# A normalised linear-attention layer and a token/channel mixer on one core: first loads in whole tiles, beta2's column beside the first channel product, q's split in two pieces, the last chunk in two halves

## The chip, the core and the metric

The kernel runs on one core of one Trainium2 chip. A core has a tensor engine (PE, with its weight loads listed apart as PEld), a vector engine (DVE), a scalar engine (ACT), GpSimd (POOL), and SyncE (SP), which here only issues DMAs; 16 DMA engines move the data. The metric is the device time of one execution in microseconds (us); the median of several executions counts.

## The reference, cut to what matters

Eight batches (`b`), 8 heads of 64 columns, 576 tokens. First an attention without softmax, with a normalised output, then a residual mixer over tokens and over channels:

```
kv  = einsum('bhsd,bhse->bhde', k, v)             # 64 x 64 per batch and head
o   = einsum('bhsd,bhde->bhse', q, kv)
x   = o / sqrt(mean(o*o, -1) + 1e-6) * g_norm     # heads side by side: 576 x 512 per batch
u   = x + lam * einsum('ts,bsd->btd', w_tok, alpha1 * x + beta1)
a2  = alpha2 * u + beta2
out = u + lam * (relu(a2 @ w_ch1) @ w_ch2)        # w_ch1: 512 x 2048, w_ch2: 2048 x 512
```

All inputs and the output are float32. The big products run in bf16.

## The kernel before

**One program, ordered by a planner.** The kernel is a list of operations, each with an engine (or two to choose from), a cost that the author wrote beside it, and the keys that it reads and writes. `plan` (L122) schedules the list eight times with due times for the first products of batch 0 and 1 (`mark`, L1277), keeps the best, and `emit` (L351) writes every engine's instructions in that order with the waits that the keys call for. Each engine runs its own list strictly in that order, so an instruction that waits holds all behind it. The author's costs decide the order alone; they have no part in the running time. Where the schedule sees PE idle before the first channel product, it puts in a **filler** (`warm`, L1341): a 128x512 matmul on zeros, whose result nobody reads. A filler is an ordinary instruction and is run whether or not PE would in fact have waited there.

**PSUM** has eight banks of 512 float32 columns; a tile takes one or two of them, and an operation that opens a tile waits for the readers of the tile before it in that bank.

**Batch 0, the start.** `load_first` (L508) loads k and v of four heads at a time: for k and for v two DMAs, each into 64 partitions (two heads, nine token rows of 64 floats to a partition, 2304 bytes in a run). `load_q` brings q's 512 first tokens of four heads, `load_tail` (L500) the last 64 tokens of all eight heads. All go through SP's queue, in the order of L1115 to L1124, with `w_tok` behind them. `kv_first` (L601) multiplies k by v in float32 on 64x64 tiles of PE, `qt_first` (L623) turns q by a product with the identity, and `qkv_groups(0)` (L745, its float32 form `f32`, L767) multiplies q by kv two heads at a time. Then come the normalisation (ACT: square L799, root L804; DVE: sum L801, reciprocal L807, scaling L820, and L824 for the token product's operand; POOL: the factor g_norm, L828), the turned `w_tok` (L1151), the token product (`tok_first`, L894), and `ut_pe` (L927), which turns u and scales it by alpha2 (L949, L950).

**The channel products.** `ch1_groups` (L976) does for each of 16 column blocks `fj` four 128x512 matmuls (even batches, L988) or eight 128x320 ones (odd batches with the tails of two batches, L1002), and ACT takes the result out of PSUM with relu (L978) and the bias `hb`, one column per `fj`. `hb` is beta2 times w_ch1: `load_w` (L1233) makes it as soon as a quarter of w_ch1 is there, with 16 matmuls of one moving column (L1256), each with its own weight load, and one copy by ACT (L1260). `ch2_groups` (L1015) multiplies by w_ch2 in parts of four matmuls (L1025); after a chunk's fourth part DVE adds u (L1035) and SP stores the chunk (L1038; the tail chunk of two batches in two DMAs, L1042). The last batch does its chunks in the order 0, 1, 2, 3, tail.

**q of the later batches.** `split_q` (L540) splits q into two bf16 parts: ACT copies it (L562, listed under L490, the line of `copy`), DVE subtracts (L564). For batches 2 to 7 that is one instruction of 128x2048 on each engine and one for the tail. `qt_dma` (L567) then turns the five token chunks by DMA transposes in SP's queue (L573), and `kv_groups` (L659) makes kv from float32 products (L673, L683), which ACT and DVE take out of PSUM (L700, L705, L708). `matmul_held` (L387) is a matmul that keeps the weights of the matmul before it: `qkv_groups` uses the pair L764 and L390 on 64 columns each.

Of the kernel before, what the change touches and what calls it, by code (L numbers as in the profile page):

```python
# [13 lines left out]
NB = 8  # L14
# [381 lines left out]
def bass_transnormer_attn__then__resmlp_affine_kernel(  # L396
# [15 lines left out]
    with ExitStack() as stack:  # L412
# [47 lines left out]
        wst = hst[:, 0:2304].rearrange("p (c s) -> p c s", c=4)  # L460
        wst2 = hst[0:64, 2304:2880]

        def nine(tile, a, g):
            return tile[64 * g:64 * g + 64, a].rearrange("p h c d -> p (h c d)")[
                :, 0:1152].rearrange("p (h c d) -> p h c d", h=2, c=9)

        def flat(ap):
            return ap.rearrange("p h d -> p (h d)")
# [31 lines left out]
        def load_tail(tile, key, src, b, lo, eng="SP"):  # L500
            P.op(eng, 0.6, lambda e: e.dma_start(
                tile[lo:lo + 64, :, :], src[b, :, 512:576, :].rearrange("h s d -> s h d")),
                w=[key], dma_us=0.75)

        HALVES = (slice(0, 4), slice(4, 8))
        ALL = (slice(0, 8),)

        def load_first(a):  # L508
            for key, src, tile in (("kf", k, kf), ("vf", v, vf)):
                for g in range(2):  # L510
                    P.op("SP", 0.45, lambda e, src=src, tile=tile, g=g: e.dma_start(
                        nine(tile, a, g).rearrange("p h c d -> p h (c d)"),
                        src[0, 4 * a + 2 * g:4 * a + 2 * g + 2].rearrange(
                            "h (p c) d -> p h (c d)", c=9)),
                        w=[(key, a)] if g == 0 else [(key + "g", a)], dma_us=1.05)

        def load_kv(b, go=()):
            j = (b + 1) % 2
            for tile, tl, src, n in ((kf, kft, k, "kf"), (vf, vft, v, "vf")):
                P.op("SP", 0.6, lambda e, tile=tile, src=src: e.dma_start(  # L520
                    tile[:, j].rearrange("p h c d -> p h (c d)"),
                    src[b, :, 0:512, :].rearrange("h (p c) d -> p h (c d)", c=4)),
                    r=go, w=[(n, j), (n + "g", j)], dma_us=3.8)
# [77 lines left out]
        def kv_first():  # L601

            def group(a):
                t = P.ptile(2)

                def f(e):
                    for c in range(9):
                        for h in (0, 2, 1, 3):
                            g, r = h // 2, slice(64 * (h % 2), 64 * (h % 2) + 64)
                            m = e.matmul(t.ap(r)[:, g, 0:64], nine(kf, a, g)[:, h % 2, c, :],  # L610
                                         nine(vf, a, g)[:, h % 2, c, :],
                                         start=(c == 0), stop=(c == 8), skip_group_check=True)
                    return m
                P.op("PE", 1.8, f, r=[(n, a) for n in ("kf", "kfg", "vf", "vfg")], w=[t])
# [8 lines left out]
        def qt_first():  # L623

            def pair(pr):
                t = P.ptile(1)

                def f(e):
                    for c in range(4):
                        for h in range(2):  # L630
                            m = e.matmul(t.flat(slice(64 * h, 64 * h + 64))[  # L631
                                :, 128 * c:128 * c + 128], qf[:, 2 * pr + h, c, :], ident[:],
                                start=True, stop=True)
                    return m
                P.op("PE", 0.95, f, r=["ident", ("qf", pr // 2)], w=[t])
# [3 lines left out]
            def tail(a):  # L639
                t = P.ptile(1)  # L640

                def f(e):
# [6 lines left out]
                P.op("PE", 0.28, f, r=["ident", "qft0"], w=[t])  # L649
# [95 lines left out]
        def qkv_groups(b):  # L745

            def group(cs, hs):
# [19 lines left out]
                def f32(e):  # L767
                    a = h0 // 4
                    for i, c in enumerate(cs):
                        for j in range(2):  # L770
                            mm = e.matmul(  # L771
                                t.flat(rows)[:, 256 * i + 128 * j:256 * i + 128 * j + 128],
                                qt32[:, 2 * a + j, 128 * c:min(128 * c + 128, 576)],
                                kv32[:, 2 * a + j, :], start=True, stop=True)
# [152 lines left out]
        def ut_pe(b):  # L927


            def group(cs, dj):  # L930
# [14 lines left out]
                al = ab2[:, 0, dj:dj + 1]  # L945

                def g(e):
                    if e is nc.scalar:
                        return e.activation(o, t.flat()[:, 0:n], ACT.Identity, scale=al)  # L949
                    return e.tensor_scalar(out=o, in0=t.flat()[:, 0:n], scalar1=al,  # L950
                                           scalar2=None, op0=ALU.mult)
# [24 lines left out]
        def ch1_groups(b):  # L976
            def relu(t, src, dst, fj, n):
                o = P.op("ACT", act_us(n) + 0.09, lambda e: e.activation(  # L978
                    dst, src(), ACT.Relu, bias=hb[:, fj:fj + 1]),
                    r=[t, ("hb", fj // 4)], w=[("ht", fj)])  # L980
                mark(b, 0, fj + 1.5, o)

            def even(fj):
                t = P.ptile(1)

                def f(e):
                    for dj in range(4):
                        m = e.matmul(t.flat(), w1[:, dj, 128 * fj:128 * fj + 128],  # L988
                                     a2t[:, dj, 0:512], start=(dj == 0), stop=(dj == 3))
                    return m  # L990
                o = P.op("PE", 0.87, f, r=[("w1", fj // 4)] + [("a2t", i) for i in range(4)],
                         w=[t])
                mark(b, 0, fj, o)
                relu(t, lambda: t.flat(), ht[:, fj, 0:512], fj, 512)

            def odd(fj):
                t = P.ptile(2)

                def f(e):
                    for i in range(2):  # L1000
# [8 lines left out]
                mark(b, 0, fj, o)  # L1009
                relu(t, lambda: t.ap()[:, :, 0:320],  # L1010
                     ht[:, fj, :].rearrange("p (a f) -> p a f", a=2), fj, 640)
            for fj in range(16):
                yield lambda fj=fj: (odd if b % 2 else even)(fj)

        def ch2_groups(b):  # L1015
            tiles = {}

            def part(c, n):
                if n == 0:
# [20 lines left out]
                else:  # L1040
                    for i in range(2):
# [3 lines left out]
            nc_ = 5 if b % 2 else 4  # L1045
            order = ([(c, n) for n in range(4) for c in range(nc_)] if b == 0
                     else [(c, n) for c in range(nc_) for n in range(4)])
            for c, n in order:
                yield lambda c=c, n=n: part(c, n)

        prow = xm[0:1, 1, :, :].rearrange("p c d -> p (c d)")
        prow2 = xtl[0:1, 1, :]
# [62 lines left out]
        for i, hs in enumerate(HALVES):  # L1115
            load_first(i)
            load_q(0, hs, False)
            if i == 0:
# [114 lines left out]
        def load_w(i):  # L1233
# [6 lines left out]
            if i < 4:  # L1240
# [9 lines left out]
                t = P.ptile(1)  # L1250

                def f(e):
                    for j in range(4):
                        fj = 4 * i + j
                        for dj in range(4):
                            m = e.matmul(t.flat()[:, j:j + 1], w1[:, dj, 128 * fj:128 * fj + 128],  # L1256
                                         b2c[:, dj:dj + 1], start=(dj == 0), stop=(dj == 3))
                    return m
# [116 lines left out]
```

## Time and profile before

| | us |
|---|---|
| device time, median of 3 (lowest, highest) | 372.38 (371.55, 372.96) |
| device time of the profiled execution | 371.84 |
| its span (first to last instruction) | 370.0 |
| PE busy within the span | 361.4 (98%) |
| DVE / ACT / POOL busy | 200.9 / 161.6 / 82.1 |
| DMA queue of SP | 92,240 packets, 59.41 MB |

The span lies 1.84 us under the device time of the same execution. A matmul's shown length holds its way through the array, so several that follow each other overlap: their pace is read from the starts, or from the chain of waits, which cuts them at the next start. "idle <- X" says how long an engine sat idle and what released it. The stages of a batch follow each other on PE with the next batch's attention laid between the channel products.

### The profile page before, as it was taken

The page shows a single profiled execution, that of the slowest core. Times are in us where ns is not written, and L with a number is a line of the kernel's source. Part 1 is how long each engine was busy: PE and PEld are TensorE (multiplying, and loading weights), DVE is VectorE, ACT ScalarE, POOL GpSimd, SP SyncE. Part 2 cuts the span into 40 slices and gives each one's busy share as a digit, 9 for nine tenths or more (in the row PEclk, how much of TensorE's full clock was granted, in tenths as well). Part 3 has the DMA queues.
Part 4 walks back from the last instruction along what each step waited for, and adds up shares of the span by engine and source line. Part 5 has one row for each costly group of instructions (what it writes and reads, how often), then busy time and mean ns, then how long its engine had stood idle before and what let it go on. Part 6 is the DMA issues. An engine that isn't in the chain of part 4 may idle for free.

```text
span 370.0 us, 7042 instructions
## 1 busy us (share of the span) xinstructions
PE 361.4 (98%) x3153; PEld 207.9 (56%) x2873; DVE 200.9 (54%) x302; ACT 161.6 (44%) x264; POOL 82.1 (22%) x69
## 2 busy tenths in 40 slices
PE   7999999999999999999999999999999999999995
PEld 3787656467754554456654554457654554457642
DVE  2377796982299279715937165925833175720021
ACT  1464886227850187008760188107730186007500
POOL 4043007340064008400341006200620007100000
PEclk9999999999999999999999999999999999999999
DMA  7999999889925893989954399233403110330021
GB/s 183 268 317 310 382 385 308 233 254 181 311 65 128 200 271 100 148 200 300 200 138 113 123 304 186 58 99 85 88 13 101 58 30 1 70 115 3 0 86 58
DMA packets 92295, 59.87 MB, mean 162 GB/s; under 512 B 59549, under 2 KB 82085, under 8 KB 92136
## 3 DMA queue, kind: packets, MB, share of 16 engines
q1 hardware_dynamic: 92240, 59.41, 61.6%
q8 instruction: 24, 0.39, 0.4%
q14 instruction: 7, 0.06, 0.1%
q10 hardware_dynamic: 24, 0.01, 0.0%
HBM read 38.56 MB, written 9.44 MB: 130 GB/s over the span
## 4 chain that ended last, share of the span: by engine, by line
PE 96%; ACT 2%; issue 0%; DVE 0%
PE ps L1025 34%; PE ps L1002 18%; PE ps L988 14%; PE ps L853 8%; PE ps L673 4%; PE ps L1342 3%; PE ps L764 2%; PE ps L390 2%; PE ps L875 1%; PE ps L771 1%; PE ps L905 1%; PE ps L940 1%; PE ps L631 1%; ACT qs L490 1%; ACT ht L978 1%; PE ps L610 1%
## 5 line engine op out<-in xcount | busy, mean ns | idle before, releaser
L1025 PE MATMUL ps<-w,ht 128*128 128x512 bf16 x576 | 129.7, 379 | 0.0
L978 ACT ACTIVATE ht<-ps,hb 128x512 bf16<-128x512 f32 (+1 forms) x128 | 93.4, 740 | 46.2 <-PE ps L1002 38.4
L828 POOL TENSOR_TENSOR xm<-xm,g_bc 128x512 f32<-128x512 f32 (+1 forms) x36 | 49.1, 1364 | 195.7 <-DVE rt L824 193.1
L1025 PEld LDWEIGHTS ps<-w,ht 128*128 128x128 bf16 x576 | 54.6, 98 | 64.3 <-issue 1.2
L1002 PE MATMUL ps<-a2t,w 128*128 128x320 bf16 x512 | 72.0, 299 | 1.4 <-ACT ht L978 1.4
L1002 PEld LDWEIGHTS ps<-a2t,w 128*128 128x128 bf16 x512 | 49.4, 98 | 21.9 <-ACT ht L978 1.9
L988 PE MATMUL ps<-a2t,w 128*128 128x512 bf16 x256 | 58.0, 379 | 0.0
L1035 DVE TENSOR_TENSOR xm<-ps,xm 128x512 f32<-128x512 f32 x32 | 21.7, 687 | 63.1 <-PE ps L1025 63.0
L700 ACT ACTIVATE kvd<-ps 64x128 bf16<-64x128 f32 x28 | 7.6, 271 | 98.0 <-PE ps L683 97.7
L801 DVE TENSOR_REDUCE small<-sq 128x16 f32<-128x1024 f32 (+3 forms) x27 | 25.2, 933 | 32.0 <-ACT sq L799 31.9
L988 PEld LDWEIGHTS ps<-a2t,w 128*128 128x128 bf16 x256 | 24.0, 98 | 26.9
L853 PE MATMUL ps<-rt,wt 128*128 128x512 bf16 x112 | 28.7, 379 | 0.0
L860 DVE TENSOR_TENSOR xm<-ps,xm 128x1024 f32<-128x1024 f32 x14 | 17.0, 1221 | 21.5 <-PE ps L853 21.4
L799 ACT ACTIVATE sq<-ps 128x1024 f32<-128x1024 f32 (+3 forms) x27 | 21.5, 797 | 8.1 <-PE ps L771 4.4
L824 DVE TENSOR_TENSOR rt<-xm,e1g_bc 128x1024 bf16<-128x1024 f32 (+1 forms) x18 | 21.3, 1182 | 0.1
L705 DVE TENSOR_TENSOR kvd<-ps,kvd 64x128 bf16<-64x128 f32 x28 | 8.1, 289 | 24.4 <-ACT kvd L700 23.8
L764 PEld LDWEIGHTS ps<-kvd,qt 128*128 128x128 bf16 x280 | 17.9, 98 | 3.9
L820 DVE TENSOR_TENSOR xm<-ps,small 128x1024 f32<-128x1024 f32 (+1 forms) x18 | 19.8, 1099 | 0.3
L564 DVE TENSOR_TENSOR qs<-qf,qs 128x2048 bf16<-128x2048 f32 (+1 forms) x10 | 17.7, 1787 | 3.1 <-ACT qs L490 3.0
L390 PE MATMUL ps<-kvd,qt 128*128 128x64 bf16 x280 | 19.0, 193 | 0.0
L764 PE MATMUL ps<-kvd,qt 128*128 128x64 bf16 x280 | 19.0, 193 | 0.0
L853 PEld LDWEIGHTS ps<-rt,wt 128*128 128x128 bf16 x112 | 11.0, 98 | 12.9 <-DVE xm L1035 0.2
(103 smaller groups left out, 287.9 us busy)
## 6 DMA issues: line engine op xcount, KB each, us to landing
out_dram<-xm SPq DMA_DIRECT2D x32, 256.0 KB, 2.6
kf<-in_k_dram SPq DMA_DIRECT2D x7, 1024.0 KB, 9.9
vf<-in_v_dram SPq DMA_DIRECT2D x7, 1024.0 KB, 9.7
qf<-in_q_dram SPq DMA_DIRECT2D x7, 1024.0 KB, 7.7
stg<-in_moe_w_ch_dram SPq DMA_DIRECT2D x3, 1024.0 KB, 14.5
kf<-in_moe_w_ch_dram SPq DMA_DIRECT2D x2, 1024.0 KB, 13.8
kf<-in_k_dram SPq DMA_DIRECT2D x4, 288.0 KB, 6.2
vf<-in_v_dram SPq DMA_DIRECT2D x4, 288.0 KB, 7.8
```

The lines of the kernel that those rows point to most:

```text
L390: return pe.add_instruction(mybir.InstMatmult(start_tensor_calc=start, stop_tensor_calc=stop, tile_size=(128, 128), tile_position=(0, 0), ...
L764: e.matmul(o, w, kvd[:, h, 0, :], start=True, stop=False)
L799: P.op("ACT", act_us(64 * m), lambda e: e.activation(sqv, raw(), ACT.Square), r=[t], w=[("sq", sqs)])
L801: P.op("DVE", dve_us(64 * m), lambda e: e.tensor_reduce(out=smv, in_=sqv.rearrange("p (h d) -> p h d", h=m), axis=AX.X, op=ALU.add), r=[(" ...
L824: lambda e: e.tensor_tensor(out=r_, in0=x, in1=eb, op=ALU.mult),
L828: P.op("POOL", pool_us(64 * nh), lambda e, xc=xc: e.tensor_tensor(out=xc, in0=xc, in1=g_bc[rows, None, :].to_broadcast([nr, nh, DH]), op=A ...
L853: m = e.matmul(t.ap()[:, i, :], tok_w(b, sc, c), rsrc(b, sc), start=(sc == 0), stop=(sc == 4))
L978: o = P.op("ACT", act_us(n) + 0.09, lambda e: e.activation(dst, src(), ACT.Relu, bias=hb[:, fj:fj + 1]), r=[t, ("hb", fj // 4)], w=[("ht", ...
L988: m = e.matmul(t.flat(), w1[:, dj, 128 * fj:128 * fj + 128], a2t[:, dj, 0:512], start=(dj == 0), stop=(dj == 3))
L1002: m = e.matmul(t.ap()[:, i, 0:320], w1[:, dj, 128 * fj:128 * fj + 128], a2t[:, dj, 320 * i:320 * i + 320], start=(dj == 0), stop=(dj == 3))
L1025: m = e.matmul(t.flat(), ht[:, fj, 128 * c:128 * c + 128], w2[:, fj, :], start=(fj == 0), stop=(fj == 15))
L1035: P.op("DVE", dve_us(512), lambda e: e.tensor_tensor(out=x, in0=t.flat(), in1=x, op=ALU.add), r=[t] + keys, w=keys)
```

## The change

In order of the diff:

- **First loads.** k and v of four heads come in one DMA each, into all 128 partitions (heads 0 and 1 of the four side by side, 2 and 3 behind them); so four DMAs for k and v in place of eight. q's last 64 tokens come in four DMAs of two heads (0 and 2, 1 and 3, and so on) in place of one of eight heads, two behind each half of q. A pair of heads in `kv32` and `qt32` is now (0, 2) or (1, 3) in place of (0, 1) or (2, 3); the float32 q·kv product writes its columns in two runs of 64.
- **q's split** for batches 2 to 7: 128x1024 twice in place of 128x2048 once, on ACT and on DVE.
- **beta2.** For batches 0 and 1 it is added where u is scaled by alpha2, so relu needs no bias there. `hb` for the later batches is made inside the first channel product of batch 0: behind each of its 64 matmuls of 512 columns stands a held matmul of one column. All 64 go to one PSUM tile that stays open for the whole product; one copy by ACT follows it.
- **The last batch's chunks** run in the order tail, 0, 1, 2, 3, and chunk 3 in two halves of 256 columns, each with its own add and its own store.

```diff
         def load_first(a):
             for key, src, tile in (("kf", k, kf), ("vf", v, vf)):
-                for g in range(2):
-                    P.op("SP", 0.45, ... nine(tile, a, g) ...
-                        src[0, 4 * a + 2 * g:4 * a + 2 * g + 2].rearrange("h (p c) d -> p h (c d)", c=9)))
+                P.op("SP", 0.6, lambda e, src=src, tile=tile: e.dma_start(
+                    nine(tile, a).rearrange("p x c d -> p x (c d)"),
+                    src[0, 4 * a:4 * a + 4].rearrange("(x y) (p c) d -> (y p) x (c d)", y=2, c=9)),
+                    w=[(key, a)], dma_us=1.6)
+        def load_first_tail(a):
+            for y in range(2):
+                P.op("SP", 0.45, lambda e, y=y: e.dma_start(
+                    qft[0:64, 4 * a + 2 * y:4 * a + 2 * y + 2, :],
+                    q[0, 4 * a + y:4 * a + y + 3:2, 512:576, :].rearrange("h s d -> s h d")),
+                    w=[("qft0", a, y)], dma_us=0.25)
...
             else:
-                parts = [((0, 1, 2, 3), ALL[0]), ((4,), ALL[0])]
+                parts = [(cs, ALL[0]) for cs in PAIRS]        # (0, 1), (2, 3), (4,)
...
                     if e is nc.scalar:
-                        return e.activation(o, t.flat()[:, 0:n], ACT.Identity, scale=al)
+                        return e.activation(o, t.flat()[:, 0:n], ACT.Identity, scale=al, bias=be)
...
         def ch1_groups(b):
-                    dst, src(), ACT.Relu, bias=hb[:, fj:fj + 1]),
-                    r=[t, ("hb", fj // 4)], w=[("ht", fj)])
+                    dst, src(), ACT.Relu, bias=hb[:, fj:fj + 1]) if b > 1 else e.activation(
+                    dst, src(), ACT.Relu), r=[t, "hb"] if b > 1 else [t], w=[("ht", fj)])
...
                     for dj in range(4):
+                        w = w1[:, dj, 128 * fj:128 * fj + 128]
+                        m = e.matmul(t.flat(), w, a2t[:, dj, 0:512], start=(dj == 0), stop=(dj == 3))
+                        if b == 0:
+                            m = P.matmul_held(hbt.flat()[:, fj:fj + 1], w, b2c[:, dj:dj + 1],
+                                              dj == 0, dj == 3)
...
+            def halves(c):
+                x = xm[:, b % 2, c, :]
+                for i in range(2):
+                    t, cols = P.ptile(1), slice(256 * i, 256 * i + 256)
+                    ... 16 matmuls of 256 columns into t, DVE adds x[:, cols], SP stores out[b, c:512:4, cols]
...
+            if b + 1 == NB:
+                order = order[16:] + order[:12]
...
-                load_tail(qft, "qft0", q, 0, 0)
+            load_first_tail(i)
...
-                P.op("PE", 0.45, f, r=["b2c", ("w1", i)], w=[t])      # 16 matmuls of one column, L1256
-                P.op("ACT", 0.2, lambda e: copy(e, hb[:, 4 * i:4 * i + 4], t.flat()[:, 0:4]),
-                     r=[t], w=[("hb", i)])
```

As the planner plays again on the new list, the order changes on every engine. On PE the built order has 45 fillers in place of 37: 23 ahead of the first k·v product (26 before) and 22 behind it in six groups (3, 1, 3, 4, 3, 8; before 11 in four groups: 2, 2, 4, 3). The group of eight stands directly ahead of the first channel product, where there was none. On SP, q of batch 5 is loaded behind the first two of batch 3's five `a2t` transposes; before, it stood behind all five, three stores and a transpose of q. On ACT, the two pieces of batch 5's q stand ahead of the copies that take batch 4's kv out of PSUM; before, the one piece stood between the fourth and the fifth relu of batch 3's channel product, behind those copies.

More of the change, by code (lines that the diff above doesn't have):

```diff
@@ L502, in load_tail @@
                 tile[lo:lo + 64, :, :], src[b, :, 512:576, :].rearrange("h s d -> s h d")),
-                w=[key], dma_us=0.75)
+                w=[key] + [("qft0", a, y) for a in range(2) for y in range(2) if lo == 0],
+                dma_us=0.75)
         HALVES = (slice(0, 4), slice(4, 8))
@@ L522, in load_kv @@
                     src[b, :, 0:512, :].rearrange("h (p c) d -> p h (c d)", c=4)),
[L523 removed]
+                    r=go, w=[(n, j)], dma_us=3.8)
                 for g in range(2):
@@ L607, in f @@
                     for c in range(9):
[L608 to L611, printed above, removed]
+                        for x, y in ((0, 0), (0, 1), (1, 0), (1, 1)):
+                            r = slice(64 * y, 64 * y + 64)
+                            m = e.matmul(t.ap(slice(64 * x, 64 * x + 64))[:, y, 0:64],
+                                         nine(kf, a)[r, x, c, :], nine(vf, a)[r, x, c, :],
                                          start=(c == 0), stop=(c == 8), skip_group_check=True)
                     return m
-                P.op("PE", 1.8, f, r=[(n, a) for n in ("kf", "kfg", "vf", "vfg")], w=[t])
+                P.op("PE", 1.8, f, r=[("kf", a), ("vf", a)], w=[t])
                 for h in range(2):
@@ L648, in f @@
                     return m
-                P.op("PE", 0.28, f, r=["ident", "qft0"], w=[t])
+                P.op("PE", 0.28, f, r=["ident"] + [("qft0", a, y) for y in range(2)], w=[t])
                 P.op(act_dve(128), 0, lambda e: copy(
@@ L771, in f32 @@
                             mm = e.matmul(
-                                t.flat(rows)[:, 256 * i + 128 * j:256 * i + 128 * j + 128],
+                                t.flat(rows)[:, 256 * i:256 * i + 256].rearrange(
+                                    "p (x y d) -> p y x d", x=2, y=2)[:, j],
                                 qt32[:, 2 * a + j, 128 * c:min(128 * c + 128, 576)],
-                                kv32[:, 2 * a + j, :], start=True, stop=True)
+                                kv32[:, 2 * a + j, :].rearrange("p (x d) -> p x d", x=2),
+                                start=True, stop=True)
                     return mm
@@ L987, in f @@
                     for dj in range(4):
-                        m = e.matmul(t.flat(), w1[:, dj, 128 * fj:128 * fj + 128],
-                                     a2t[:, dj, 0:512], start=(dj == 0), stop=(dj == 3))
-                    return m
-                o = P.op("PE", 0.87, f, r=[("w1", fj // 4)] + [("a2t", i) for i in range(4)],
-                         w=[t])
+                        w = w1[:, dj, 128 * fj:128 * fj + 128]
+                        m = e.matmul(t.flat(), w, a2t[:, dj, 0:512],
+                                     start=(dj == 0), stop=(dj == 3))
+                        if b == 0:
+                            m = P.matmul_held(hbt.flat()[:, fj:fj + 1], w, b2c[:, dj:dj + 1],
+                                              dj == 0, dj == 3)
+                    return m
+                hbt = hts[0] if b == 0 else None
+                o = P.op("PE", 0.87 if b else 0.91, f, r=[("w1", fj // 4)]
+                         + [("a2t", i) for i in range(4)] + ["b2c"] * (b == 0),
+                         w=[t] + [hbt] * (b == 0))
                 mark(b, 0, fj, o)
@@ L1011, in odd, with f @@
                      ht[:, fj, :].rearrange("p (a f) -> p a f", a=2), fj, 640)
+            hts = [P.ptile(1)]
             for fj in range(16):
                 yield lambda fj=fj: (odd if b % 2 else even)(fj)
+            if b == 0:
+                yield lambda: P.op("ACT", 0.2, lambda e: copy(e, hb[:], hts[0].flat()[:, 0:16]),
+                                   r=[hts[0]], w=["hb"])
         def ch2_groups(b):
             tiles = {}
+            def halves(c):
+                x = xm[:, b % 2, c, :]
+                for i in range(2):
+                    t, cols = P.ptile(1), slice(256 * i, 256 * i + 256)
+                    def f(e, t=t, cols=cols):
+                        for fj in range(16):
+                            m = e.matmul(t.flat()[:, 0:256], ht[:, fj, 128 * c:128 * c + 128],
+                                         w2[:, fj, cols], start=(fj == 0), stop=(fj == 15))
+                        return m
+                    P.op("PE", 1.74, f, r=[("w2", n) for n in range(4)]
+                         + [("ht", n) for n in range(16)], w=[t])
+                    keys = [xkeys(b, c)[i]]
+                    P.op("DVE", dve_us(256), lambda e, t=t, cols=cols: e.tensor_tensor(
+                        out=x[:, cols], in0=t.flat()[:, 0:256], in1=x[:, cols], op=ALU.add),
+                        r=[t] + keys, w=keys)
+                    P.op("SP", 0.6, lambda e, cols=cols: e.dma_start(
+                        out[b, c:512:4, cols], x[:, cols]), r=keys, dma_us=0.5)
             def part(c, n):
```

30 lines of the change are left out of this document (10 added, 20 removed).

## The prediction

> **What bounds the kernel now.** I read the page first, for which engine is busy, then the busy time in stretches, for where PE is not, then the waits and the chain, for why.
>
> ```profile
> PE 361.4 (98%) x3153; PEld 207.9 (56%) x2873; DVE 200.9 (54%) x302; ACT 161.6 (44%) x264; POOL 82.1 (22%) x69
> ```
> ```profile
> 0.00:60.00 60.00, 57.43 (x673) 38.47 (x658) 38.67 (x80) 34.37 (x70) 16.67 (x26) 1.00 1.03 309
> ...
> 120.00:180.00 60.00, 58.63 (x572) 32.51 (x490) 34.88 (x48) 28.49 (x46) 12.43 (x8) 1.00 0.89 203
> ...
> 300.00:370.00 70.00, 65.35 (x381) 34.27 (x363) 21.73 (x28) 23.32 (x34) 8.13 (x6) 1.00 0.15 46
> ```
>
> PE is idle for 8.6 of 370.0 us, and these three stretches hold all of it (the second number is PE's busy time): 2.57, 1.37 and 4.65 us. So outside of a few gaps the time is the sum of what PE's list holds, and an edit counts by what it adds to that list, by the gaps that it opens or closes, and by the end behind the last matmul. The gaps inside:
>
> ```profile
> PE ps L1002 <- ACT ht L978: 1.4, 1, 1.4
> ...
> PE ps L1256 <- ACT w L490: 0.5, 1, 0.5
> ...
> PE ps L610 <- issue: 0.2, 1, 0.2
> ```
>
> The first stretch's other 1.9 us lie ahead of PE's first matmul. A gap costs more than it shows, since a matmul's shown length goes on after the next could have started:
>
> ```profile
> 176.52 0.45 PE L1002 MATMUL ps<-a2t,w 128*128 128x320 bf16 x2 [1.37 <-ACT ht L978]
> ```
> ```profile
> 170.02 0.03 PE ps L764
> ...
> 170.96 1.10 PE ps L1002 x8
> ```
>
> Eight of L1002 follow each other in 1.10 us, 0.14 each, but two are shown with 0.45 us, so the last is shown with 0.31: 0.17 more than its pace. With that I count the three gaps as 1.55, 0.65 and 0.4 us.
>
> ```profile
> 19.14 0.54 PE ps L1342 x2
> ...
> 31.37 0.65 PE ps L1342 x3
> 32.02 2.62 PE ps L905 x24
> ...
> 49.47 0.38 PE ps L1256 x16
> ...
> 365.39 0.69 DVE xtl L1035
> ```
>
> These rows of the chain give the prices. Three fillers among bf16 matmuls take 0.65 us, 0.217 each; two beside float32 matmuls of another tile shape take 0.54, so a change of shape costs 0.1. A matmul of 256 columns takes 2.62/24 = 0.109 us. Sixteen one-column matmuls with their weight loads take 0.38 us, 0.024 each. The end is DVE's add, the stores and their landing.
>
> **The change part by part.** The sum is made against the profiled execution's own 371.84 us (span 370.0 and 1.84 outside it), which lies 0.54 under the median of 372.38; the same difference is then taken from the median.
>
> *Fillers, through the reordering: +1.73 us, and +0.1.* The built order has 45 in place of 37, and PE runs each wherever it stands: 8 x 0.217. One more change of tile shape stands in the new order by my count of the groups. That no real matmul waits in their place is what the rest of the start must show.
>
> *First loads: 0 by themselves.*
>
> ```profile
> 4.00:5.00 1.00, 1.00 (x4) 0.43 (x3) 0.00 (x0) 0.00 (x0) 0.88 (x3) 1.00 1.04 225
> ```
> ```profile
> 37.00:46.00 9.00, 8.51 (x135) 5.90 (x134) 6.83 (x13) 7.17 (x16) 0.00 (x0) 1.00 1.05 382
> ```
> ```profile
> 2.22 1.28 SPq L511 DMA_DIRECT2D vf<-in_v_dram  x2
> ```
> ```profile
> 9.54 1.14 PEld L610 LDWEIGHTS ps<-vf,kf 64*64 64x64 f32 x72 [0.42 <-DMA vf<-in_v_dram]
> ```
>
> The DMA engines are full in both windows (share 1.04 and 1.05), but move 225 GB/s (last number) with the loads into 64 partitions and 382 with loads into 128. The first four heads of k and v are 1.18 MB: 5.2 us at the one rate, 3.1 at the other. Today v of them releases PE at 9.5 us; 2.1 us less, or the same at worst. PE gets to its first product behind 23 fillers, 3 x 0.217 earlier, at about 8.8 us; at worst it waits 0.5 us for v there. Everything behind the second four heads moves up by some 4 us (2 x 2.1), so the loads of batch 1 and of w_ch1 come earlier as well. q's tails are four issues in place of one, but k and v are four fewer (0.64 us each, by the row above), so SP's queue is no longer. Yet an earlier product gains nothing in the end, since its fillers are merely counted later.
>
> *The start's chain:* with the new order I followed each PE group's waits up to the token product of batch 1 with the durations of the same instructions. None comes out late. The closest is the first channel product: behind the last turned u stand 1.73 us of fillers, and ACT needs two a2t copies and one kv copy in that time.
>
> ```profile
> 36.35 1.84 ACT L949 ACTIVATE a2t<-ps,ab 128x512 bf16<-128x512 f32 x3 [4.53 <-PE ps L940]
> ```
> ```profile
> 165.86 1.13 ACT L700 ACTIVATE kvd<-ps 64x128 bf16<-64x128 f32 x4 [19.66 <-PE ps L683]
> ```
>
> That is 2 x 0.61 + 0.28, 1.5 us; so the fillers cover it with 0.2 to spare. beta2 inside that copy is an operand more of the same instruction, and relu without the bias the same instruction: 0 each.
>
> *beta2's column: +0.1 us (0 to +0.35).* Out go 64 one-column matmuls at 0.024 us, 1.54 us. In come 64 held ones. Their price isn't shown; the nearest rows are those 0.024 us with a weight load, and the held pairs of q·kv on 64 columns:
>
> ```profile
> L764 PEld LDWEIGHTS ps<-kvd,qt 128*128 128x128 bf16 x280 | 17.9, 98 | 3.9
> ```
> ```profile
> 55.28 0.19 PE L764 MATMUL ps<-kvd,qt 128*128 128x64 bf16 x1
> 55.31 0.19 PE L390 MATMUL ps<-kvd,qt 128*128 128x64 bf16 x1
> 55.34 0.19 PE L764 MATMUL ps<-kvd,qt 128*128 128x64 bf16 x1
> ```
>
> A start every 0.03 us, with a 98 ns weight load every 0.06: the next weights come in beneath the held matmul. So 64 x 0.024 to 64 x 0.03. A rule speaks against this: the Trainium skill, TensorE: Matmul & The Clock Gate, Part 3, says that a weight load overlaps matmuls in flight only where it goes to another row group. By it each held column would leave a load bare; the sum with that stands among the rivals. The trace disagrees with it by the 58 ns of these pairs, all on the whole array.
>
> *The gap at w_ch1's second quarter: -0.65 us.* PE waited for ACT's cast (0.5 us in the waits). The new order puts 16 matmuls of batch 1's q·kv ahead of the block that needs it, and the load lies some 4 us earlier; by my walk the cast is done over 1 us before. Gone; at worst it stays. The 0.4 us "issue" gap in the second k·v group has no producer behind it; I let it stay (-0.4 to 0).
>
> *q in two pieces: -1.55 us.*
>
> ```profile
> 172.77 1.90 ACT L490 ACTIVATE qs<-qf 128x2048 bf16<-128x2048 f32 x1
> ```
> ```profile
> 153.07 6.54 SPq L970 DMA_TRANSPOSE a2t<-a2b  x5
> ```
> ```profile
> 163.24 0.43 SPq L494 DMA_DIRECT2D qf<-in_q_dram  x1
> ```
> ```profile
> DMA to landing us min/median/max: 6.4/7.7/11.7
> ```
>
> ACT copies batch 5's q, 1.9 us, in the middle of batch 3's relus, and PE runs out of free PSUM. In the new order both pieces stand ahead of the kv copies at 165.86 (quoted above), in an idle time of 19.66 us. They need q, whose load (L494, landing 6.4 to 11.7 us after its issue) now stands behind two a2t transposes: 153.1 + 2 x 1.31, about 155.7 in place of 163.2. It lands at about 163.4, the two pieces end near 165.5, and the kv copies start as they do today. Two more copies and two more subtractions for each of six batches cost a little each, on engines busy for about half the time: 0.
>
> *The end: -0.85 us, and +0.02.*
>
> ```profile
> L820 DVE TENSOR_TENSOR xtl<-ps,small 64x256 f32<-64x256 f32 x2 | 0.8, 412 | 0.0
> ```
> ```profile
> 366.11 1.13 SPq L1042 DMA_DIRECT2D out_dram<-xtl  x2
> ```
>
> The last add is of 256 columns, 0.41 us in place of 0.69, and one issue stands behind it in place of two (0.56 each). The other half's add and store lie beside 16 matmuls. 32 matmuls of 256 columns take 3.49 us, 16 of 512 at the fillers' pace 3.47. The landing is bounded by today's and, with half the bytes behind it, 0.3 us less; I take today's.
>
> **Sum:** 1.73 + 0.1 + 0.1 - 0.65 - 1.55 - 0.85 + 0.02 = -1.1 us. 371.84 becomes 370.7, and the median **371.3 us** (-0.3%). A difference under 0.5%, 1.86 us, is about what a measurement of this kernel can't tell from none.
>
> **The rivals.**
>
> - *Faster by over 0.5%: 370.4 us.* The "issue" gap goes (-0.4), the one-column matmuls cost less than those with a load (-0.2), the last store lands 0.25 us sooner: -1.95. For it: the loads that the issue gap may come from are over earlier. Against it: three small things must come together. 18%.
> - *The relu gap stays: 372.9 us.* Batch 3's relus have a q tail and three squares among them still; if they alone emptied PSUM, the 1.55 us are lost. Against it: batch 5, with no q among its relus, shows no gap. 15%.
> - *New waits at the start: 372.3 us.* The order of 60 us is new and the slack ahead of the first channel product is 0.2 us: v late by 0.5, a copy late by 0.5. 12%.
> - *Slower: q of batch 5 comes late, 375.8 us.* Its pieces now stand ahead of batch 4's kv copies. Today those start at 165.86, DVE's part behind them ends at 168.65, and the q·kv product that needs it starts at 170.02 us:
>
> ```profile
> 168.19 0.46 DVE L708 COPY kvd<-kvd 64x256 bf16<-64x256 bf16 x2
> ```
>
>   So there are 1.3 us of slack, and from a landing at about 165.5 on every us later costs PE one; at 167 the gain is gone. If SP is held up so that the load goes out where it does today, at 163.2, it lands at 170 to 171, and PE waits some 4.5 us. The row of landings speaks against it: even 11.7 us from 155.7 is 167.4. 8%.
> - *Slower: the held column keeps the next weights out, 377.6 us.* 64 x 0.098 = 6.3 us. The pairs above speak against it. 3%. It is the page's rule on row groups that would give this time.
>
> **How the numbers follow.** The forecast has 44%. Faster by over 0.5%: the first rival and a little of the forecast's edge, 0.21. Slower by over 0.5%: the last two, and 0.02 of the others' edges, 0.13. Within: 0.66. The range reaches over the first three rivals with their edges, 369.9 to 373.2, and leaves out the two slow ones and the far ends.
>
> **What would show it.** 45 fillers, and first k·v product near 8.8 us with the DMA rate over 300 GB/s before it; the first channel product some 1.3 us later than today, with a pace of 0.24 us per pair of 512 and one column; the token product of batch 1 0.6 to 1.2 us later than today; no PE gap at batch 3's relus, and from there PE earlier than today; 3.8 us from the last matmul's end to the span's end in place of 4.6. Wrong would be: a wait for q (L494) on ACT ahead of the kv copies, a pace over 0.28 us in the first channel product, or a new releaser of PE in the first 60 us.

## The result, and the profile after

| | before | after |
|---|---|---|
| device time, median of 16 runs (lowest, highest), us | 372.24 (371.30, 372.96) | 371.01 (370.24, 371.92) |
| ratio, with its 95% interval | 1 | 0.9967 (0.9959 to 0.9975) |
| device time of the profiled execution, us | 371.84 | 371.58 |
| its span, us | 370.0 | 369.5 |

The change makes the kernel faster by 0.33%, 1.23 us; the forecast was 371.3 us, and 1.1 us less. The interval is 0.08% to either side, so 16 runs of each kernel do tell this difference from none; the prediction had put that limit at 0.5%. But the two profiled executions differ by 0.26 us only, so the traces have to be read with care.

The page of the changed kernel: busy time, share of the span and number of instructions per engine.

```profile
PE 364.1 (99%) x3177; PEld 208.8 (56%) x2833; DVE 200.3 (54%) x303; ACT 161.7 (44%) x270; POOL 80.7 (22%) x72
```

PE's busy time in the same stretches as before (second number):

```profile
0.00:60.00 60.00, 58.14 (x692) 37.49 (x599) 36.33 (x72) 34.16 (x68) 22.50 (x31) 1.00 1.03 326
...
120.00:180.00 60.00, 59.81 (x576) 32.75 (x494) 38.50 (x55) 28.99 (x48) 9.49 (x7) 1.00 0.89 214
...
300.00:370.00 70.00, 66.14 (x416) 36.48 (x389) 22.14 (x29) 24.09 (x35) 8.10 (x6) 0.99 0.17 47
```

PE is idle for 1.86 us in place of 2.57 in the first stretch, which is now only the time ahead of its first matmul, and for 0.19 in place of 1.37 in the third. (The last stretch reaches 0.5 us past this span's end.) PE's waits, all of them:

```profile
PE ps L1371 <- DVE a2b L1168: 1.9, 1, 1.9
PE ps L1017 <- ACT ht L987: 0.2, 1, 0.2
```

The wait for w_ch1's second quarter and the "issue" gap are gone, and of the wait at batch 3's relus 0.2 us is left. The chain of waits gives the start, first one row of the kernel before, then the changed kernel:

```profile
1.86 5.55 PE ps L1342 x18
```
```profile
1.86 7.51 PE ps L1371 x23
...
15.06 1.21 PE ps L617 x72
...
39.99 1.73 PE ps L1371 x8
41.72 0.22 PE ps L998
41.94 0.24 PE ps L998
```

The second k·v product (72 matmuls) now takes 1.21 us in one piece, where it had a hole (shown as 0.21, counted as 0.4). A pair of 512 and one held column takes 0.24 us, 0.2414 by the starts. And the first rows hold a surprise: the first 18 fillers in one piece took 5.55 us before, 23 take 7.51 now. At 0.2163 us each, the pace of those behind, that would be 3.89 and 4.97 us. By the intervals between their starts, the first 8 or so of before ran at about 0.427 us each, and the first 12 of after, though both began at 1.86 us. This alone is 0.88 us between the two traces. How long that slow spell is differs from run to run, as the experiments below show; it explains most of why two single executions differ by less than the medians do.

Landmarks on PE, from the chains of both kernels, in us:

| | before | after | difference | less 0.88 |
|---|---|---|---|---|
| first k·v product starts | 9.61 | 9.73 | +0.12 | -0.76 |
| first channel product starts | 39.18 | 41.72 | +2.54 | +1.66 |
| batch 1's channel product | 84.02 | 85.82 | +1.80 | +0.92 |
| batch 3's channel product | 166.76 | 168.69 | +1.93 | +1.05 |
| PE goes on after its stall there | 176.52 | 177.27 | +0.75 | -0.13 |
| last matmuls done, last add starts | 365.39 | 366.18 | +0.79 | -0.09 |
| span's end | 370.0 | 369.5 | -0.5 | -1.38 |

So the start costs 0.9 us (it loses the gaps and gains fillers), the stall in batch 3 gives 1.2 back, and the end gives 1.3.

### The profile page after: what moved, and what is told of

It reads as the page before. It is cut to its first block, busy times and chain, and to the rows that moved or that the text cites. A ratio compares the mean times of both kernels' runs of the same rounds, so it can differ in the third digit from the quotient of the medians.

```text
span 369.5 us, 7029 instructions
## 1 busy us (share of the span) xinstructions
PE 364.1 (99%) x3177; PEld 208.8 (56%) x2833; DVE 200.3 (54%) x303; ACT 161.7 (44%) x270; POOL 80.7 (22%) x72
## 4 chain that ended last, share of the span: by engine, by line
PE 97%; ACT 1%; issue 0%; DVE 0%
PE ps L1063 33%; PE ps L1017 18%; PE ps L998 15%; PE ps L862 8%; PE ps L680 4%; PE ps L1371 3%; PE ps L390 2%; PE ps L771 2%; PE ps L778 1%; PE ps L884 1%; PE ps L914 1%; PE ps L949 1%; PE ps L638 1%; PE ps L1044 1%; PE ps L690 1%; PE ps L1202 1%
## 5 line engine op out<-in xcount | busy, mean ns | idle before, releaser
L1063 PE MATMUL ps<-w,ht 128*128 128x512 bf16 x560 | 126.6, 379 | 0.0
L987 ACT ACTIVATE ht<-ps,hb 128x512 bf16<-128x512 f32 (+1 forms) x96 | 70.3, 740 | 42.0 <-PE ps L1017 35.7
L1063 PEld LDWEIGHTS ps<-w,ht 128*128 128x128 bf16 x560 | 53.0, 98 | 62.4 <-issue 1.2
L837 POOL TENSOR_TENSOR xm<-xm,g_bc 128x512 f32<-128x512 f32 (+1 forms) x36 | 45.2, 1254 | 195.5 <-DVE rt L833 193.8
L998 PE MATMUL ps<-a2t,w 128*128 128x512 bf16 x256 | 59.5, 378 | 0.0
L988 ACT ACTIVATE ht<-ps 128x512 bf16<-128x512 f32 (+1 forms) x32 | 20.6, 650 | 8.3 <-PE ps L1017 4.6
L571 DVE TENSOR_TENSOR qs<-qf,qs 128x1024 bf16<-128x1024 f32 (+1 forms) x16 | 18.9, 1210 | 7.0 <-ACT qs L490 7.0
L490 ACT ACTIVATE qs<-qf 128x1024 bf16<-128x1024 f32 (+1 forms) x14 | 13.4, 987 | 15.8 <-DMA qf<-in_q_dram 14.2
L833 DVE TENSOR_TENSOR rt<-xm,e1g_bc 128x1024 bf16<-128x1024 f32 (+1 forms) x17 | 19.8, 1167 | 0.2
L390 PE MATMUL ps<-kvd,qt 128*128 128x64 bf16 x280 | 19.2, 193 | 0.0
```

The lines of the kernel that those rows point to most:

```text
L390: return pe.add_instruction(mybir.InstMatmult(start_tensor_calc=start, stop_tensor_calc=stop, tile_size=(128, 128), tile_position=(0, 0), ...
L837: P.op("POOL", pool_us(64 * nh), lambda e, xc=xc: e.tensor_tensor(out=xc, in0=xc, in1=g_bc[rows, None, :].to_broadcast([nr, nh, DH]), op=A ...
L987: o = P.op("ACT", act_us(n) + 0.09, lambda e: e.activation(dst, src(), ACT.Relu, bias=hb[:, fj:fj + 1]) if b > 1 else e.activation(dst, sr ...
L988: dst, src(), ACT.Relu, bias=hb[:, fj:fj + 1]) if b > 1 else e.activation(
L998: m = e.matmul(t.flat(), w, a2t[:, dj, 0:512], start=(dj == 0), stop=(dj == 3))
L1063: m = e.matmul(t.flat(), ht[:, fj, 128 * c:128 * c + 128], w2[:, fj, :], start=(fj == 0), stop=(fj == 15))
```

## The experiments

Each is told as a ratio to the kernel before on the same chip; a thousandth is 0.37 us. The changed kernel stands at 0.9967. Where the kernel's own order is to be kept, instructions are left out or moved behind the planner:

```
P.plan(due, 8)
gone = set(fillers[2:10])          # which, differs from run to run
... an operation that depends on one that is gone takes over its dependencies
P.sequence = [o for o in P.sequence if o not in gone]
```

### Eight fillers fewer ahead of the first k·v product

`gone = set(fillers[2:10])`, of 23.

> The changed kernel in its own order, with 8 of the 23 fillers ahead of the first k·v product left out. In its trace v has landed at 6.05 us, and PE comes to the product at 9.7 us. My theory: fillers that stand ahead of no late operand are paid in full, so the whole program moves up by 8 x 0.217 = 1.73 us, 369.3 us in place of 371.0. Rival: the start is bound by loads further back (q, w_tok, w_ch1), PE waits for one of them instead, and the time stays at 371.0 us. On the clock: if the slow spell of PE at the start is a stretch of time that begins anywhere, its length in this trace has nothing to do with the number of fillers: between 3 and 7 us; if it counted matmuls, 8 or 12 slow fillers would show again.

Measured: 0.9919 (0.9906 to 0.9932), median 369.43 us. Against the changed kernel that is 0.0048, 1.8 us for eight fillers, with an uncertainty of about 0.6 us; PE waits for no load. The theory holds: v has landed at about 6.0 us, and what stands ahead of PE's first product is paid in full. The slow spell held 9 fillers here, 12 in the changed kernel, about 8 in the kernel before.

### Without the eight fillers ahead of the first channel product

`gone = set(fillers[37:45])`

> The changed kernel in its own order without the group of eight fillers that stands directly ahead of the first channel product. My theory (the prediction's walk): ACT needs 1.5 us there for two a2t copies and one kv copy, so 1.5 of the 1.73 us become a wait of PE for a2t, and the time falls by 0.2 us at most, 370.8 us. Rival: the fillers cover nothing and the time falls by 1.7 us, 369.3 us.

Measured: 0.9963 (0.9952 to 0.9975), median 370.82 us, 0.15 us less than the changed kernel. PE's waits in this kernel:

```profile
PE ps L998 <- ACT a2t L958: 1.6, 1, 1.6
```

A wait of 1.6 us has taken the place of 1.73 us of fillers. So equal instructions at two places of one list are worth 1.8 and 0.15 us.

### Without any filler behind the first product

`gone = set(fillers[23:])`

> The changed kernel in its own order without any of the 22 fillers behind the first k·v product (4.8 us). My theory: most of them stand where a copy out of PSUM or a normalisation is not yet done, PE waits there instead, and 1 to 2 us are gained: 369 to 370 us, with waits of PE of 2.5 us or more in the first 45 us. Rival: they cover nothing, and the time is 4.8 us less, 366.2 us. A third: without them PE rests long enough for its clock to fall, and the time is not lower than 371 us.

Measured: 0.9970 (0.9951 to 0.9989), median 372.09 us: nothing gained for 4.8 us of work left out. The third theory came closest for most runs. PE's waits and the stretches around the first channel product:

```profile
PE ps L390 <- ACT a2t L958: 2.2, 1, 2.2
```
```profile
38.00:42.00 4.00, 1.79 (x14) 1.12 (x11) 2.76 (x6) 3.92 (x10) 0.00 (x0) 0.94 1.05 384
42.00:46.00 4.00, 4.00 (x31) 2.14 (x23) 2.03 (x6) 3.35 (x6) 1.49 (x2) 0.63 1.05 386
```

PE rests before 41.1 us, and then its granted clock (the third number from the end) falls to 0.63 of full over 42 to 46 us. Of eleven runs, seven have a mean clock of 0.994 or 0.995 over the whole program and take 371.7 to 372.5 us; the other four have 0.998 to 1.0 and take 369.4 to 370.3, about what the first theory said. So the fillers do two things: they fill a wait, and they keep the clock up through it. The Trainium skill, TensorE: Matmul & The Clock Gate, Part 1, names an idle window of about 3.4 us as what lowers the clock. Here 2.2 us of idle time was enough in the profiled run, and by their mean clocks in six others.

### q's split undone

```diff
-                parts = [(cs, ALL[0]) for cs in PAIRS]
+                parts = [((0, 1, 2, 3), ALL[0]), ((4,), ALL[0])]
```

> The changed kernel with q's split undone: one piece of 128x2048 for batches 2 to 7. PE's list is the same; on ACT the piece of batch 5 stands between the fourth and the fifth relu of batch 3 again. My theory: that place was the stall. In the traces it cost 1.53 us before and 0.35 us after, so the time goes up by 1.2 us, 372.2 us, and PE waits for a relu at about 175 us again. Rival: the stall went because the whole start is different, and the time stays at 371.0 us.

Measured: 0.9998 (0.9988 to 1.0009), median 372.22 us, 1.15 us more than the changed kernel. The wait is back:

```profile
PE ps L1017 <- ACT ht L987: 1.4, 1, 1.4
```

### One piece, in the place of the two

ACT's two copies of batch 5's q are made one of 128x2048 at the first one's place in the finished order.

> The changed kernel in its own order, but ACT's two pieces of batch 5's q are one copy of 128x2048 at the first piece's place, ahead of batch 4's kv copies. My theory: what counts is the place, not the length of a piece; 1.90 us there in place of 2 x 0.99, 371.0 us as the changed kernel. Rival: a long piece is what stalls PE, and the time is that of one piece in the old place, 372.2 us.

Measured: 0.9967 (0.9954 to 0.9980), median 370.97 us, the same as the changed kernel. So it is the place that counts. Two pieces matter because with them the planner comes to another order; a long piece ahead of the kv copies does no harm.

### beta2 as before

The edit takes back the diff's part on beta2: no bias in `ut_pe`, the bias in every relu, 16 one-column matmuls per quarter of w_ch1.

> The changed kernel with beta2 as before: relu with bias in batches 0 and 1, hb from 16 one-column matmuls per quarter with weight loads of their own. The planner gives 43 fillers in place of 45. My theory: the held columns cost what the others did (64 x 0.025 in the trace of the changed kernel, 64 x 0.024 before), so only the two fillers count: 371.0 - 0.43 = 370.6 us. Rival: the blocks of hb bring the wait for w_ch1's second quarter back, +0.65: 371.2 us or more.

Measured: 0.9952 (0.9940 to 0.9964), median 370.35 us: 0.56 us faster than the changed kernel, though the two intervals overlap. At 0.217 us each the two fillers would be 0.43 of it. No wait for w_ch1 came back, though the blocks did. So the held columns are not what closed that gap, and no gain from them shows here.

### The first loads as before

The edit takes back all of the diff that concerns the first loads.

> The changed kernel with the first loads of before (eight DMAs into 64 partitions, one tail). The planner gives 47 fillers in place of 45, 26 of them ahead of the first k·v product. My theory: the loads count only through the fillers and the gap inside the second k·v product: 371.0 + 0.43 + 0.4 at most, 371.4 to 371.8 us. Rival: v lands 3 us later and everything behind it follows, 373 us or more.

Measured: 1.0078 (1.0057 to 1.0100), median 375.59 us: 4.1 us slower than the changed kernel, and slower than the kernel before. My theory is wrong by far, and the rival has the size but not the place. Until the first channel product (41.43 us, against 41.72) nothing is late. PE's wait is a new one, and the stretches around it:

```profile
PE ps L1054 <- DVE w L1291: 2.2, 1, 2.2
```
```profile
64.00:68.00 4.00, 1.84 (x8) 0.62 (x7) 4.00 (x5) 0.00 (x0) 2.12 (x2) 0.96 1.08 268
68.00:72.00 4.00, 4.00 (x13) 1.58 (x12) 3.64 (x6) 0.29 (x1) 0.00 (x0) 0.62 0.39 94
```

L1291 scales w_ch2 for the second channel product, in pieces on POOL and DVE. POOL's first piece begins when its load lands:

```profile
49.83 4.64 POOL L1291 TENSOR_TENSOR w<-stg,lam_bc 128x512 bf16<-128x512 f32 x3 [4.21 <-DMA stg<-in_moe_w_ch_dram]
```

In the changed kernel the same wait ends at 46.12 us, 3.7 earlier:

```profile
46.12 1.28 POOL L1299 TENSOR_TENSOR w<-stg,lam_bc 128x512 bf16<-128x512 f32 x1 [1.50 <-DMA stg<-in_moe_w_ch_dram]
```

But the later load doesn't explain the wait. In the kernel before it goes out at the same time (the first three quarters from 37.38 us in both) and lands at the same time (the third quarter at 54.94 us, here at 55.19), and no wait follows. What differs is where the scaling stands on DVE. These are DVE's first pieces in the kernel before, and here:

```profile
50.86 4.89 DVE L1270 TENSOR_TENSOR w<-stg,lam_bc 128x512 bf16<-128x512 f32 x8
```
```profile
59.78 1.89 DVE L1291 TENSOR_TENSOR w<-stg,lam_bc 128x512 bf16<-128x512 f32 x3
```

In the kernel before, DVE scales eight pieces from 50.86 us on, ahead of batch 1's normalisation. Here the planner's new order lays the sums and scalings of that normalisation first, and a copy that waits 0.8 us for PE; DVE comes to w_ch2 at 59.78 us, 4.6 us after the third quarter has landed, while POOL rests for 8.4 us behind its three pieces. PE stands at 65 us, rests 2.2 us, and its clock falls to 0.62 for the next stretch. Again the clock counts for about as much as the wait: two of the six runs keep a mean clock of 1.0, and take 373.6 and 374.1 us; four have 0.995 and 375.5 to 376.2. So the wait, and with it most of the 4.1 us, goes with the order that the planner makes for the old loads. What the loads alone would cost in an unchanged order, no run shows.

### The first loads alone

The kernel before with nothing but the new first loads.

> The kernel before with the first loads of the change and nothing else of it. The planner gives 43 fillers in place of 37. My theory: the earlier landing is worth nothing of itself, the plan spends it on fillers: +6 x 0.217, less the two gaps of the start (w_ch1's second quarter 0.65, the gap in the second k·v product 0.4), +0.25 us: 372.5 us. Rival: the loads are what made the change faster, and alone they bring 371 us or less.

Measured: 1.0016 (1.0007 to 1.0026), median 372.77 us, 0.6 us slower than before. As expected, and a little worse: six fillers more, the wait for w_ch1 gone, the stall in batch 3 as before. With the order that the planner makes for them, the faster loads bring no time of their own.

### The last batch's chunks as before

```diff
-            if b + 1 == NB:
-                order = order[16:] + order[:12]
...
-            if b + 1 == NB:
-                yield lambda: halves(3)
```

> The changed kernel with the last batch's chunks in the order of before (0, 1, 2, 3, tail) and no halves; the start is the same. By the trace of the changed kernel the end shrank from 4.6 to 3.3 us: 1.3 us longer, 372.3 us. By the prediction's term the end is worth 0.85 us, and the other 0.45 us of that trace are scatter of the last store's landing: 371.85 us.

Measured: 0.9996 (0.9988 to 1.0005), median 372.27 us. The end is worth 0.0029, 1.1 us: between the trace's 1.3 and the prediction's 0.85.

### The new order of chunks, chunk 3 whole

```diff
-                order = order[16:] + order[:12]
+                order = order[16:] + order[:16]
...
-            if b + 1 == NB:
-                yield lambda: halves(3)
```

> The changed kernel with the last batch's new order of chunks (tail first), but chunk 3 whole: one add of 512 columns and one store of 256 KB at the end. The end of the change was worth 1.26 us. My theory: the order is worth about half of it (one store behind the last add in place of two, 0.53 us by the issues), the halves the rest (0.27 us of add and some of the landing): 371.0 + 0.6 = 371.6 us. Rival: it is all in the order (371.0 us); or all in the halves (372.3 us).

Measured: 0.9980 (0.9970 to 0.9989), median 371.28 us: 0.5 us more than with halves, 0.6 less than the old end. Both parts count. The last adds of the three kernels (before, this one, the changed one):

```profile
365.39 0.69 DVE L1035 TENSOR_TENSOR xtl<-ps,xtl 128x512 f32<-128x512 f32 x1 [2.76 <-PE ps L1025]
```
```profile
365.12 0.69 DVE L1073 TENSOR_TENSOR xm<-ps,xm 128x512 f32<-128x512 f32 x1 [2.76 <-PE ps L1063]
```
```profile
366.18 0.42 DVE L1050 TENSOR_TENSOR xm<-ps,xm 128x256 f32<-128x256 f32 x1 [1.32 <-PE ps L1044]
```

From the add's end to the span's end (370.0, 369.1, 369.5) it is 3.92, 3.29 and 2.90 us. By these single traces 0.63 us go with the one issue less, another 0.39 with half the bytes in the last store, and the add is 0.27 shorter.

### The terms put together

The kernel with beta2 as before, 8 of its 22 first fillers left out, and the tail copy of batch 5's q moved behind batch 3's seventh relu.

> The change without its part on beta2 (370.35 us), without 8 of the fillers ahead of the first k·v product, and with the tail copy of batch 5's q moved behind batch 3's seventh relu on ACT, its subtraction behind a normalisation on DVE. If the terms add: 370.35 - 1.73 - 0.35 = 368.3 us, with no wait of PE near 175 us. Rival: the earlier start meets a load further back (w_ch1 or w_ch2), and the time stays above 369 us.

Measured: 0.9896 (0.9881 to 0.9911), median 368.41 us (367.74 to 368.97), 1.0% less than before. The terms add to within 0.1 us (the interval is 0.6 us to either side), PE doesn't wait near 175 us, and the version beats both kernels.

### More fillers left out

As the last, but 26 of 43 fillers out, and ACT's kv copies behind its a2t copies.

> As the kernel with the terms added, but 26 of the 43 fillers left out in place of 8 (12 ahead of the first k·v product, 8 spread behind it, 6 of the 8 ahead of the first channel product), and ACT's kv copies behind its a2t copies. 18 x 0.217 = 3.9 us more are to be had, 364.4 us, if no wait stands behind any of them; my theory expects waits for about half, 366.4 us. Rival: the waits grow long enough for PE's clock to fall, as it did in most runs without any late filler, and the time is 368 us or more in such runs.

Measured: 0.9904 (0.9873 to 0.9935), median 367.90 us. Of six runs four take 367.2 to 368.0 and two 370.7 and 370.8; the profiled one is of the long kind. Its waits behind the first matmul stay small (the longest 0.4 us), so the rival is right on the price and wrong on the place. This is its chain at the start:

```profile
7.04 2.13 PE ps L618 x72
...
11.17 3.61 PE ps L639 x32
...
15.36 0.38 PE ps L1376
15.74 1.21 PE ps L618 x72
```

The first k·v product takes 2.13 us, the second 1.21; the turned q takes 3.61 us, against 1.90 in the kernel before. PE is at about half pace until about 15 us. In this run ten fillers were not enough to raise the clock, and the small float32 matmuls behind them didn't raise it either. That the other run of 370.8 us is long for the same reason is likely, but not shown.

## Why the prediction was right, point by point

- **Fillers, +1.73: right.** 0.217 us each by the chain, 0.22 by the eight left out. That no product waits in their place at the first one, and that 1.5 of 1.73 us are needed at the first channel product, both came out (nothing there; 1.6).
- **First loads, 0 by themselves: no gain alone, as said; their worth within the change is open.** With nothing else of the change the kernel is 0.6 us slower than before. Taking them from the change costs 4.1, but through the order that the planner then makes: DVE comes to w_ch2 at 59.8 us, long after it has landed. For the order that was built, the step's walk held: no wait for a load appeared.
- **beta2's column, +0.1: right.** 64 x (0.2414 - 0.2163) is 1.6 us, against 1.54. No weight load stands bare: the row-group rule of the Trainium skill (TensorE: Matmul & The Clock Gate, Part 3), taken alone, does not hold for these pairs. The pace of 0.2414 us leaves 0.025 for the held column, where a bare load would add 0.098.
- **The gap at w_ch1's second quarter, -0.65: right in size; of its two reasons, the load is not the one.** The cast that PE waited for doesn't end earlier but later, at 47.94 us in place of 45.38. The last casts of that quarter, before and after:

```profile
44.32 1.06 ACT L490 ACTIVATE w<-w 128x1024 bf16<-128x1024 f32 x1
```
```profile
46.26 1.68 DVE L491 CAST w<-w 128x1024 bf16<-128x1024 f32 x1
```

  What moved is PE, which comes to the first product on this quarter at 48.13 us in place of 45.85: the channel product starts later, and batch 1's q·kv stands ahead of that block. The cast is done 0.2 us before it is needed, where the walk had over 1 us. With beta2 as before, or with the first loads as before, the cast ends at 45.49 or 46.01 us and PE comes at 46.50 or 47.51; neither kernel waits there.
- **The "issue" gap, 0 (at best -0.4): it went.** No cause is shown: the kernel with q's split undone has the same list on PE up to there, and shows a hole of 0.34 us at 16.4 us where the changed kernel has none.
- **q in two pieces, -1.55: right in place, 0.37 too large.** The load went out at 156.9 us (expected 155.7), landed at 162.8 (163.4), and the pieces were over ahead of the kv copies. (It is one more copy and one more subtraction a batch, not two as the step says.) What the step left out is the q tail and a square that still stand among the relus. The changed kernel's chain there:

```profile
173.97 0.63 ACT qs L490
174.63 0.79 ACT ht L987
175.42 0.91 ACT sq L808
176.33 0.19 ACT small L813
176.53 0.69 ACT ht L987
177.22 0.05 issue
177.27 1.26 PE ps L1017 x8
```

  By the starts 0.35 us of stall are left, so 1.18 are gained. The rival "the relu gap stays" had named these two; it was right for less than a quarter of it. With the tail's copy moved there is no wait.
- **The end, -0.85: right in kind, too small.** 1.29 us in the trace, 1.1 by the runs. The landing was taken as unchanged; in the traces it is 0.4 us shorter with half the bytes.
- **Not in the sum: the slow spell of PE's first matmuls.** The sum was made against one execution, which had 8 slow fillers; the changed kernel's had 12. Where the prediction said what the trace would show, it was wrong for this: the first product at 9.73 us and not near 8.8, the first channel product 2.5 us later and not 1.3, and PE still later than before behind batch 3. Less 0.88 us the first would be at 8.85 us, as said, and PE 0.13 us earlier behind batch 3; but the first channel product is still 1.66 us later. A part of batch 1's k·v (16 matmuls, 0.39 us) now stands ahead of it, which stood behind it before. The DMA rate was as expected (406 GB/s in the fifth microsecond).

With the measured sizes the sum is 1.73 + 0.1 + 0.07 - 0.65 - 0.4 - 1.18 - 1.29 + 0.02 = -1.6 us, against -1.38 in the spans less the slow spell, and -1.23 in the medians. (The 0.1 for a change of tile shape was not measured.) Of the 0.2 between sum and spans, 0.13 lies between batch 1's and batch 3's channel products, and wasn't followed. That the forecast met the median to 0.3 us is in part luck, errors of both signs: 0.4 too little for the issue gap, 0.4 too much for q, 0.4 too little for the end.

## What to carry to other kernels

- A filler is worth what stands behind it: ask for each group which wait would take its place, and leave out those that have none. Where one has, a wait of some 2 us may cost as much again through the clock.
- A part of a change that makes a planner come to another order can't be priced by taking it out: what the run then shows may be the price of the new order. Where the same operands land at the same time and only one of two kernels waits for them, look at the lists of the engines and not at the load.
- Before two traces are subtracted, compare a stretch that should be equal in both, such as the first matmuls.

## What was not expected of the hardware

The same 23 fillers, all beginning at 1.86 us, took between 6.43 and 7.85 us in seven kernels that have them in one row (6.43, 6.54, 6.99, 7.30, 7.51, 7.58, 7.85), and the change to full pace came between 4.7 and 7.4 us. The Trainium skill, TensorE: Matmul & The Clock Gate, Part 1, says that the window which raises the clock runs free and doesn't start with the kernel; these runs agree. As an estimate, this spread of 1.4 us would make most of the spread of the sixteen runs of either kernel (1.66 and 1.68 us). The granted clock in the stretches reads 1.00 through this first spell, so it has to be read from the starts of the matmuls; later falls, as at 42 and at 68 us above, it does show.
